# Gate-row loads on ScalarE and GpSimd, sixteen copies on three engines, and a half step more before a visit

## The chip, the cores and the metric

The kernel runs on one core of a Trainium2 chip. The time is device microseconds of one execution; the lower, the better. A profile is one execution taken by the hardware profiler, with a record for each instruction and each DMA packet. In it PE is the tensor engine's matmuls, PEld its weight loads, DVE is VectorE, ACT is ScalarE, POOL is GpSimd, SP is SyncE, and SPq, ACTq and so on are the engines' sequencers (for a DMA: the issue).

## The reference

An attention block without softmax, and on its output a mixture of four experts. All is float32.

```python
def phi(x):                                   # (4, 4, 1088, 32) -> 64 features
    a = einsum('rd,bhsd->bhsr', S1, x)        # S1, S2: (8, 32)
    b = einsum('rd,bhsd->bhsr', S2, x)
    return einsum('bhsi,bhsj->bhsij', a, b).reshape(..., 64)
q_p, k_p = phi(q), phi(k)
kv, z = einsum('bhsf,bhsd->bhfd', k_p, v), k_p.sum(axis=2)
attn = einsum('bhsf,bhfd->bhsd', q_p, kv) / (einsum('bhsf,bhf->bhs', q_p, z) + 1e-6)
x = attn.transpose(0, 2, 1, 3).reshape(4352, 128)
p = domain_probs / (domain_probs.sum(-1) + 1e-9)          # (4352, 4)
out = sum(p[:, e:e+1] * (maximum(x @ w1[e], 0) @ w2[e]) for e in range(4))
# w1: (4, 128, 1024), w2: (4, 1024, 128)
```

## The kernel before

**Tokens and chunks.** The 4352 tokens are cut into eleven chunks: 128, 448, 512, seven of 448, and 128 (`CHUNKS`). For each chunk the expert part runs 16 steps (`NQ`): four experts, four steps each, a step being two blocks of 128 hidden columns. So there are 176 steps, of two half steps each. The first and last chunk are done with plain float32 matmuls in halves (`plain`, L245); chunk 1 uses plain float32 for its first expert (L1102); all the others use three float32r products per block (L1115, L1116, L1164), from weights split into parts (`wa`, `wb`, `wd` by `weight_parts`; `vab`, `vb`, `vd` by `second_weight_parts`) and tokens split into `xa`, `xb`, `xd`. ScalarE takes the relu (`hid` at L1093, L1104, L1172, or `ha` at L1167), VectorE makes the low parts `hb` (L1141) and `hd` (L1144). The second matmuls (`o`, L245, L1213, L1232) follow two steps and more behind.

**Order.** The schedule is written by hand: every engine runs its instructions in the order in which the program emits them, and semaphores make it wait for the others. The main loop is over steps. Work of the attention for later tokens stands as small pieces in a list, `plan`, and `work()` takes pieces from it at each half step, as a credit allows. A piece may have a condition `(name, n)`: it isn't taken before n half steps after the piece `name` ran. `until_there` forces pieces when a chunk's tokens are due.

**The start.** `start()` does the keys and values of the first batch and the first 128 queries (`x_first`), on which the first chunk's step 0 waits. Loads are issued by SP in program order: `S2`, keys `kn`, 128 queries, values `vn` (six loads), 448 queries, `w1` of expert 0, then the gate rows `dp` (three loads, L187) and `ends` (two, L192), then the weights of all experts, the last queries, and the second batch's keys and values. `S1` alone is issued by ScalarE. `gate_sums`, on GpSimd, is the first reader of `dp` and `ends`.

**The second unit.** `queries` and `attend` make the 448 tokens of chunk 1 during chunk 0. Their pieces are `first0` to `first17`: VectorE's shuffles and products (`qp`, L582), the visit on PE (`h<-kvx,qp`), the division, the transpose into `y` (L698), and the copies from `y` to the four row groups of `ring` (L710): sixteen copies of 32 rows and 96 or 128 columns, in two rounds `first16` and `first17`, today on ScalarE (odd heads) and GpSimd (even heads):

```python
copy = nc.scalar.copy if h % 2 else nc.gpsimd.tensor_copy
```

**Later units.** Ten units (`later`) make the rest of the tokens. Each goes: turn on VectorE, projection on PE (`h<-qT,sx`), copy `qs` on ScalarE, out to DRAM and back (`qd`), two products on VectorE (L780), and a visit: the next unit's projection, then this unit's `h<-kvx,qp`. The visit's condition is a number of half steps behind the second product.

Of the kernel before, what the change touches and what calls it, by code (L numbers as in the profile page):

```python
# [17 lines left out]
def _ap(t, p0: int, np_: int, off: int, free):  # L18

    p = list(t.ap)[0]  # L20
    return bass.AP(t.tensor, t.offset + p0 * p[0] + off, [[p[0], np_]] + [list(d) for d in free])
# [3 lines left out]
def kernel(  # L25
# [24 lines left out]
    nc = tc.nc  # L50

    P = 128
    HP = 64
    B, H, S, D = q.shape
    E, DM, F = w1.shape
    R = 8
    R2 = 2 * R
    G = S // 32
# [80 lines left out]
    def load_w1(e):  # L139
        w1_of[e] = cpool.tile([P, F], F32, tag=f"w1_{e}", name="w1_sb")  # L140
        for c in (slice(0, F // 2), slice(F // 2, F)) if e == 1 else (slice(0, F),):
            nc.sync.dma_start(w1_of[e][:, c], w1[e, :, c])

    def load_w2(e, k, to=None):
        of = OTHER if k else THREE
        w2_of[e, k] = cpool.tile([P, len(of) * DM], F32, tag=f"w2_{e}{k}", name="w2_sb")[:, :] if to is None else to
        runs = []
        for b in of:
            if runs and b == runs[-1][1]:
                runs[-1][1] += 1  # L150
            else:
                runs.append([b, b + 1])
        for b, z in runs:
            at = split_at(b)
            nc.sync.dma_start(  # L155
                w2_of[e, k][:, DM * at : DM * (at + z - b)].rearrange("p (g d) -> p g d", d=DM),
                w2[e, P * b : P * z].rearrange("(g p) d -> p g d", p=P),
            )
# [21 lines left out]
    dp = cpool.tile([P, G, E], F32, name="dp")  # L180

    ends = cpool.tile([P, 2, E], F32, name="ends")
    e_sum = cpool.tile([P, 2, 3], F32, name="e_sum")
    load_rows(q, 0, "qn", slice(P, P + UNITS[0][1]))
    load_w1(0)
    for p0, n, g0, m, t in ((0, 96, 0, G, 0), (96, 32, 0, G - 4, 3 * S), (96, 32, G - 4, 4, B * S - P)):
        nc.sync.dma_start(  # L187
            _ap(dp, p0, n, g0 * E, [[1, m * E]]),
            bass.AP(domain_probs.tensor, domain_probs.offset + t * E, [[m * E, n], [1, m * E]]),
        )  # L190
    for i, t, g in ((0, 0, G), (1, B * S - P, 4)):
        nc.sync.dma_start(  # L192
            ends[:, i, :], bass.AP(domain_probs.tensor, domain_probs.offset + t * E, [[g * E, 32], [1, 4 * E]])
        )
    load_w2(0, 0)
    load_w2(0, 1)
    for e in range(1, E):
# [89 lines left out]
    def copy_on(scalar):  # L287
        return nc.scalar.copy if scalar else nc.gpsimd.tensor_copy
# [7 lines left out]
        )  # L296
    for h in range(H):
        copy_on(h > 1)(_ap(sr, 32 * h, 32, 32 * h, [[P, 6], [1, 32]]), _ap(sp, 0, 32, 0, [[32, 6], [1, 32]]))
    mask_lo = [R2 + l % R2 for l in range(32)]
    mask_b = [R + l % R for l in range(32)]  # L300
    mask_a = [[4 * x + l // R for l in range(32)] for x in range(2)]
# [69 lines left out]
    def placed(c, n):  # L371

        for a, z, t, off in PLACES:
            lo, hi = max(c, a), min(c + n, z)
            if lo < hi:
                yield t[:, off + lo - a : off + hi - a], lo - c, hi - lo
# [317 lines left out]
    def attend_out(b, c, n, laid, xs):  # L694

        y = apool.tile([P, QW], F32, tag="y", name="y")
        for c0, T, t0 in laid:
            nc.vector.transpose(  # L698
                _ap(y, 0, P, P * t0, [[32, T[0]], [32 * T[0], H], [1, 32]]),
                _ap(xs, 0, P, P * t0, [[P, T[0]], [D, H], [1, D]]),  # L700
            )
            if b == 0 and c == P:
                for x in range(2):
                    yield
                    for a in (x, x + 2):
                        run = 32 * T[a // 2]
                        for h in range(H):
                            copy = nc.scalar.copy if h % 2 else nc.gpsimd.tensor_copy
                            at = PLACES[1][3] + a // 2 * 64 * T[0] + a % 2 * run
                            copy(ring[32 * h : 32 * h + 32, at : at + run], _ap(y, 32 * a, 32, 32 * T[0] * h, [[1, run]]))  # L710
                continue
            m = 64 * sum(T)
            base = xd.offset + P * (S * b + c + c0)
            for a in range(4):
                run = 32 * T[a // 2]
                nc.sync.dma_start(
                    bass.AP(
                        xd.tensor,
                        base + a // 2 * 64 * T[0] + a % 2 * run,
                        [[m, 32], [32 * m, H], [1, run]],  # L720
                    ),
                    _ap(y, 32 * a, 32, P * t0, [[32 * T[0], H], [1, run]]),
                )
            for to, at, w in placed(S * b + c + c0, m):
                nc.sync.dma_start(to, bass.AP(xd.tensor, base + at, [[m, P], [1, w]]))
        have[0] += n
        yield
# [71 lines left out]
    def add(cost, run, name, after=None):  # L799

        plan.append((cost, run, name, after))

    def lay_plan():

        of_first = queries(0, P, UNITS[0][1])
        costs = [0.62] * 9 + [0.05] * 4 + [0.4, 0.55, 0.6, 0.1, 0.1]
        distances = {12: ("first8", 3), 13: ("first12", 1), 16: ("first15", 2), 17: ("first16", 1)}
        for at, cost in enumerate(costs):
            add(cost, lambda: next(of_first, None), f"first{at}", distances.get(at))
        covers.append((len(plan), P + UNITS[0][1]))  # L810
        add(vector_us(later[0][2]), lambda: unit_turn(0), "qturn", ("start", 2 * NQ - 2))
        add(0.1, lambda: unit_project(0), "visit", ("qturn", 6))
        add(0, lambda: None, "wait", ("start", 2 * NQ + 2))
        keys = {}
        for b in range(1, B):
            now_on, plan[:] = list(plan), []
            key_pieces(b)
            keys[b], plan[:] = list(plan), now_on
        for w, (b, c, n, u) in enumerate(later):
            if b == 0:  # L820
                plan.extend(keys[1][:9])
            else:
                at = {(1, 0): (1, 9, 13), (1, 1): (2, 0, 3), (1, 2): (2, 3, 5), (2, 0): (2, 5, 13)}
                at.update({(2, 1): (3, 0, 3), (2, 2): (3, 3, 9), (3, 0): (3, 9, 13)})
                if (b, u) in at:
                    k, z0, z1 = at[b, u]
                    plan.extend(keys[k][z0:z1])
                if u == 0:
                    key_end(b)
            more = w + 1 < len(later)  # L830
            if more:
                add(vector_us(later[w + 1][2]), lambda w=w: unit_turn(w + 1), "qturn")
            for p in range(2):
                add(vector_us(n), lambda w=w, p=p: unit_product(w, p), "product", ("visit", LAND if w else LAND + 1))

            def visit(w=w, more=more):
                if more:
                    unit_project(w + 1)
                unit_visit(w)

            add(0.1, visit, "visit", ("product", 3 if w < 4 else 2))
            add(0.4, lambda w=w: inverse.__setitem__(w, attend_inverse(*products[w])), "inverse", ("visit", 1))
            add(vector_us(n), lambda w=w: over.__setitem__(w, attend_scale(*products[w], inverse.pop(w))), "scale")
            add(vector_us(n), lambda w=w: unit_out(w), "out")
            covers.append((len(plan), S * b + c + n))
# [3 lines left out]
    def queries(b, c, n):  # L849
        qc = early.pop((b, c))  # L850
        qf = apool.tile([P, QW], F32, tag="qf", name="qf")
        nc.vector.stream_shuffle(in_=qc[:, 0:n], out=qf[:, 0:n], mask=mask_lo)
        yield
        nc.vector.tensor_tensor(out=qf[:, 0:n], in0=qc[:, 0:n], in1=qf[:, 0:n], op=ALU.add)
        free()
        yield
        qb = apool.tile([P, QW], F32, tag="qb", name="qb")
        nc.vector.stream_shuffle(in_=qf[:, 0:n], out=qb[:, 0:n], mask=mask_b)
        yield
        qp = query_tiles()  # L860
        for x in range(2):
            qa = apool.tile([P, QW], F32, tag="qa", name="qa")
            nc.vector.stream_shuffle(in_=qf[:, 0:n], out=qa[:, 0:n], mask=mask_a[x])
            yield
            for p in range(2):
                query_product(qp, p, x, n, qa, qb)
                yield
        yield
        yield
        yield  # L870
        yield from attend(b, c, n, qp)
# [460 lines left out]
    for m in range(1, NC - 1):  # L1332
        at, tokens = NQ * m - 4 if m > 1 else NQ + 1, token_parts(m)
# [45 lines left out]
    for i in range(len(steps) + LA):  # L1379
        if i < len(steps):  # L1380
            m, kq = steps[i]
# [84 lines left out]
```

## Time and profile before

| | us |
|---|---|
| median of three runs (453.1 to 453.74) | 453.47 |
| the profiled execution | 454.41 |
| its span, first to last instruction | 452.6 |

| engine | busy us | share | instructions |
|---|---|---|---|
| PE | 445.4 | 98% | 3013 |
| PEld | 367.8 | 81% | 3013 |
| DVE | 357.0 | 79% | 600 |
| ACT | 332.0 | 73% | 703 |
| POOL | 119.2 | 26% | 206 |

The span is cut into 40 slices of 11.3 us, and each digit is a busy share in tenths: PE shows 8 in the first slice, 7 in the last, and 9 in all others. The granted TensorE clock is full in all. The DMA engines moved 38.45 MB, a mean of 85 GB/s, with up to 283 GB/s in the second slice. In the chain of work that ended last, PE holds 90%, ACT, DMA and the SP queue 2% each.

Rows of the timeline read: start, duration, engine, line, operation, output<-input, shape, count, and in brackets the idle time before the first of them with what ended it. Rows of the same kind that follow each other are merged, so the duration is from the first start to the last end.

### The profile page before, as it was taken

How to read it: one execution, taken by the hardware profiler on the slowest of the kernel's cores; microseconds unless marked ns; L12 is line 12 of the kernel's file. 1: busy time of each engine (PE TensorE's matmuls, PEld its weight loads, DVE VectorE, ACT ScalarE, POOL GpSimd, SP SyncE). 2: the span in 40 equal slices, each digit the busy share in tenths (PEclk: the TensorE clock that was granted, in tenths of full speed). 3: DMA queues.
4: the chain of work that ended last, by engine and by line, in shares of the span. 5: the costliest groups of instructions: out<-in, count | busy, mean ns of one | idle time of the engine just before them, and what ended most of it. 6: DMA issues, size and time to landing. Idle time of an engine off the chain costs nothing.

```text
span 452.6 us, 8664 instructions
## 1 busy us (share of the span) xinstructions
PE 445.4 (98%) x3013; PEld 367.8 (81%) x3013; DVE 357.0 (79%) x600; ACT 332.0 (73%) x703; POOL 119.2 (26%) x206
## 2 busy tenths in 40 slices
PE   8899999999999999999999999999999999999997
PEld 5776678777778888788888888888888888888886
DVE  5868679887988788788877998788779787887753
ACT  4276888777867786688687867787778788878841
POOL 6344133310333123212221232124123212321320
PEclk9999999999999999999999999999999999999999
DMA  6964741114313350151243501320321121017401
GB/s 179 283 172 136 181 123 55 36 23 131 98 46 90 80 136 25 32 135 63 73 116 52 141 22 28 102 67 21 84 61 23 38 45 43 20 37 221 149 2 28
DMA packets 54003, 38.45 MB, mean 85 GB/s; under 512 B 27144, under 2 KB 50120, under 8 KB 53960
## 3 DMA queue, kind: packets, MB, share of 16 engines
q1 hardware_dynamic: 53560, 37.85, 30.9%
q8 instruction: 23, 0.38, 0.3%
q14 instruction: 20, 0.16, 0.1%
q0 software_dynamic: 384, 0.06, 0.1%
q10 hardware_dynamic: 16, 0.00, 0.0%
HBM read 32.68 MB, written 5.21 MB: 84 GB/s over the span
## 4 chain that ended last, share of the span: by engine, by line
PE 90%; ACT 2%; DMA 2%; SPq 2%; DVE 1%; issue 1%; DVEq 0%; ACTq 0%
PE o L1232 39%; PE h L1164 13%; PE h L1115 12%; PE h L1116 12%; PE h L245 7%; PE o L245 2%; PE o L1213 2%; PE h L1102 1%; PE h L430 1%; DMA w_sb<-in_moe_w_dram 1%; SPq L155 1%; DMA vn<-in_v_dram 1%; ACT h L1117 1%; ACT vab L887 0%; ACT ring L710 0%
## 5 line engine op out<-in xcount | busy, mean ns | idle before, releaser
L1117 ACT ACTIVATE h<-h 128x448 f32<-128x448 f32 (+1 forms) x280 | 151.4, 541 | 78.2 <-PE h L1116 73.9
L1141 DVE SCALAR_TENSOR_TENSOR hb<-h,ha 128x448 fp32r<-128x448 f32 (+1 forms) x204 | 125.8, 624 | 53.5 <-ACT ha L1167 52.5
L1115 PE MATMUL h<-xa,wa 128*128 128x448 f32 (+1 forms) x280 | 130.4, 466 | 0.0
L1144 DVE SCALAR_TENSOR_TENSOR hd<-ha,hb 128x896 fp32r<-128x896 f32 (+1 forms) x102 | 116.4, 1141 | 8.5 <-PE h L245 0.5
L1167 ACT ACTIVATE ha<-h 128x448 fp32r<-128x448 f32 (+1 forms) x204 | 111.7, 548 | 0.0
L1164 PE MATMUL h<-xd,wd 128*128 128x448 f32 (+1 forms) x280 | 103.7, 370 | 0.6 <-ACT h L1117 0.6
L1116 PE MATMUL h<-xb,wb 128*128 128x448 f32 (+1 forms) x280 | 103.1, 368 | 0.0
L1271 POOL TENSOR_TENSOR ev<-ev,gate 128x256 f32<-128x256 f32 (+1 forms) x54 | 39.3, 727 | 220.2 <-DVE ev L1264 202.0
L1232 PE MATMUL o<-ha,vab 128*128 128x448 f32 (+1 forms) x204 | 76.3, 374 | 0.0
L1115 PEld LDWEIGHTS h<-xa,wa 128*128 128x128 f32 x280 | 52.7, 188 | 18.7 <-issue 14.3
L1116 PEld LDWEIGHTS h<-xb,wb 128*128 128x128 f32 x280 | 52.7, 188 | 18.6 <-issue 14.8
L1232 PE MATMUL o<-hid,w_sb 128*128 128x448 f32 (+1 forms) x136 | 62.9, 544 | 0.0
L1164 PEld LDWEIGHTS h<-xd,wd 128*128 128x128 f32 x280 | 52.5, 187 | 9.2 <-ACT h L1117 2.7
L1232 PE MATMUL o<-hd,vd 128*128 128x448 f32 (+1 forms) x204 | 58.8, 369 | 0.0
L1232 PE MATMUL o<-hb,vb 128*128 128x448 f32 (+1 forms) x136 | 50.0, 369 | 0.0
L1273 POOL TENSOR_TENSOR total<-total,ev 128x256 f32<-128x256 f32 (+1 forms) x54 | 47.3, 876 | 4.2
L1172 ACT ACTIVATE hid<-h 128x448 f32<-128x448 f32 (+1 forms) x76 | 42.2, 555 | 0.1
L1232 PEld LDWEIGHTS o<-ha,vab 128*128 128x128 f32 x204 | 38.3, 188 | 4.1 <-issue 0.2
L1232 PEld LDWEIGHTS o<-hd,vd 128*128 128x128 f32 x204 | 38.0, 188 | 3.5
L1271 POOL TENSOR_TENSOR total<-ev,gate 128x256 f32<-128x256 f32 (+1 forms) x18 | 12.8, 730 | 78.6 <-issue 58.6
L1232 PEld LDWEIGHTS o<-hid,w_sb 128*128 128x128 f32 x136 | 25.6, 188 | 2.2
L1232 PEld LDWEIGHTS o<-hb,vb 128*128 128x128 f32 x136 | 25.5, 188 | 2.2
(140 smaller groups left out, 451.2 us busy)
## 6 DMA issues: line engine op xcount, KB each, us to landing
gate<-gates SPq DMA_DIRECT2D x24, 224.0 KB
kn<-in_k_dram SPq DMA_DIRECT2D x4, 544.0 KB
vn<-in_v_dram SPq DMA_DIRECT2D x16, 128.0 KB
w_last<-in_moe_w_dram SPq DMA_DIRECT2D x4, 512.0 KB
w_sb<-in_moe_w_dram SPq DMA_DIRECT2D x3, 512.0 KB
w_sb<-in_moe_w_dram SPq DMA_DIRECT2D x6, 256.0 KB
qp<-qd SPq DMA_DIRECT2D x6, 224.0 KB
qb<-qd SPq DMA_DIRECT2D x6, 224.0 KB
```

The lines of the kernel that those rows point to most:

```text
L245: nc.tensor.matmul(out(s), weights(s), moving(s), **flags)
L1115: nc.tensor.matmul(g, wa[:, e, w], xa, start=True, stop=False)
L1116: nc.tensor.matmul(g, wb[:, e, w], xb, start=False, stop=True)
L1117: nc.scalar.activation(g, g, ACTF.Copy, scale=1.0 + R12)
L1141: nc.vector.scalar_tensor_tensor(out=hb, in0=g, scalar=0.0, in1=high, op0=ALU.max, op1=ALU.subtract)
L1144: nc.vector.scalar_tensor_tensor(out=d2, in0=a2.bitcast(F32), scalar=R12, in1=b2.bitcast(F32), op0=ALU.mult, op1=ALU.subtract)
L1164: nc.tensor.matmul(g, w, x, start=False, stop=True, skip_group_check=True)
L1167: nc.scalar.activation(ha, g, ACTF.Relu, scale=NEAR)
L1172: nc.scalar.activation(hid[i][j], g, ACTF.Relu)
L1232: nc.tensor.matmul(acc[m, e][o][:, 0:n], w, h, start=first_one, stop=last)
L1271: nc.gpsimd.tensor_tensor(out=to[:, x], in0=ev[:, x], in1=g[:, x], op=ALU.mult)
L1273: nc.gpsimd.tensor_tensor(out=total[m][:, x], in0=total[m][:, x], in1=ev[:, x], op=ALU.add)
```

## The change

Three edits. First, the five loads of gate rows leave SP's queue, where they stood between the first expert's `w1` and `w2`, and are emitted later in the program, after the copies that build `sr`: the three of `dp` on ScalarE, the two of `ends` on GpSimd. Second, the sixteen copies to `ring` are dealt to VectorE (six), GpSimd (six) and ScalarE (four), and the second round waits two half steps after the first instead of one. Third, the visit of a later unit waits three half steps behind its second product for all units; before it was two for the fifth and later ones.

```diff
     load_rows(q, 0, "qn", slice(P, P + UNITS[0][1]))
     load_w1(0)
-    for p0, n, g0, m, t in ((0, 96, 0, G, 0), (96, 32, 0, G - 4, 3 * S), (96, 32, G - 4, 4, B * S - P)):
-        nc.sync.dma_start(
-            _ap(dp, p0, n, g0 * E, [[1, m * E]]),
-            bass.AP(domain_probs.tensor, domain_probs.offset + t * E, [[m * E, n], [1, m * E]]),
-        )
-    for i, t, g in ((0, 0, G), (1, B * S - P, 4)):
-        nc.sync.dma_start(
-            ends[:, i, :], bass.AP(domain_probs.tensor, domain_probs.offset + t * E, [[g * E, 32], [1, 4 * E]])
-        )
     load_w2(0, 0)
...
     for h in range(H):
         copy_on(h > 1)(_ap(sr, 32 * h, 32, 32 * h, [[P, 6], [1, 32]]), _ap(sp, 0, 32, 0, [[32, 6], [1, 32]]))
+    for p0, n, g0, m, t in ((0, 96, 0, G, 0), (96, 32, 0, G - 4, 3 * S), (96, 32, G - 4, 4, B * S - P)):
+        nc.scalar.dma_start(
+            _ap(dp, p0, n, g0 * E, [[1, m * E]]),
+            bass.AP(domain_probs.tensor, domain_probs.offset + t * E, [[m * E, n], [1, m * E]]),
+        )
+    for i, t, g in ((0, 0, G), (1, B * S - P, 4)):
+        nc.gpsimd.dma_start(
+            ends[:, i, :], bass.AP(domain_probs.tensor, domain_probs.offset + t * E, [[g * E, 32], [1, 4 * E]])
+        )
...
-                            copy = nc.scalar.copy if h % 2 else nc.gpsimd.tensor_copy
+                            at = "vgsvgvsg"[a // 2 * H + h]
+                            copy = {"v": nc.vector.tensor_copy, "g": nc.gpsimd.tensor_copy, "s": nc.scalar.copy}[at]
...
-        distances = {12: ("first8", 3), 13: ("first12", 1), 16: ("first15", 2), 17: ("first16", 1)}
+        distances = {12: ("first8", 3), 13: ("first12", 1), 16: ("first15", 2), 17: ("first16", 2)}
...
-            add(0.1, visit, "visit", ("product", 3 if w < 4 else 2))
+            add(0.1, visit, "visit", ("product", 3))
```

## The prediction

> **What bounds the kernel now.** I read the summary of busy time first (PE 445.4 of 452.6 us, granted clock 1.000 throughout), so only a stretch in which PE stands still can be won. The next view is who PE waited for. Its three lines that this change can reach:
>
> ```profile
> PE h L245 <- DMA w_sb<-in_moe_w_dram: 0.9, 1, 0.9
> PE o L245 <- ACT hid L1093: 0.7, 1, 0.7
> PE h L245 <- DVE qp L780: 0.3, 1, 0.3
> ```
>
> Columns: total us, times, longest. A PE row ends later than the next could start (a 128-column row shows 0.27 us, yet back to back they start 0.04 to 0.07 apart), so I price each stall from start to start. The timeline, first around 20 us:
>
> ```profile
> 19.71 0.62 DVE L582 TENSOR_TENSOR qp<-qa,qb 64x448 f32<-64x448 f32 x1
> 20.36 0.35 DVE L1196 TENSOR_SCALAR end<-o,ends 128x128 f32<-128x128 f32 x1
> 20.73 0.62 DVE L582 TENSOR_TENSOR qp<-qa,qb 64x448 f32<-64x448 f32 x1
> 21.22 0.66 PE L245 MATMUL h<-x_first,w_sb 128*64 128x128 f32 x8 [0.94 <-DMA w_sb<-in_moe_w_dram]
> 21.68 1.13 PE L245 MATMUL h<-kvx,qp 128*64 128x66 f32 x32
> 22.61 0.64 PE L245 MATMUL o<-w_sb,hid 128*64 128x128 f32 x8
> ```
>
> The row before 21.22 starts at 20.01; the next was due at 20.07. PE lost 1.15 us waiting for the third expert's first weights (step 8). Then ScalarE's copies:
>
> ```profile
> 25.07 2.35 ACT L710 COPY ring<-y 32x128 f32<-32x128 f32 x8
> 27.44 0.66 ACT L1093 ACTIVATE hid<-h 128x256 f32<-128x256 f32 x2
> 27.88 0.66 PE L245 MATMUL o<-w_sb,hid 128*64 128x128 f32 x8 [0.70 <-ACT hid L1093]
> ```
>
> Eight copies in a row hold back a `hid` that PE wants at 26.95: 0.93 us. Third, the visit of the fifth unit:
>
> ```profile
> 189.36 0.42 DVE L780 TENSOR_TENSOR qp<-qp,qb 128x256 f32<-128x256 f32 x1
> 189.83 0.45 PE L245 MATMUL h<-kvx,qp 128*64 128x66 f32 x8 [0.26 <-DVE qp L780]
> ```
>
> The row before starts at 189.34, so 0.49 less the usual 0.03: 0.46 us. From 300 us on PE repeats one expert of a 448-column chunk every 10.02 us, and visits add only their own work; nothing later takes back time won earlier, as due times count half steps and move with PE. The most to be had is 1.15 + 0.93 + 0.46 = 2.54 us.
>
> **Part 1, the gate loads leave SP.** The issue queue shows what stood ahead of those weights:
>
> ```profile
> 5.58 0.35 SPq L109 DMA_DIRECT2D qn<-in_q_dram  x1
> 5.98 0.43 SPq L142 DMA_DIRECT2D w_sb<-in_moe_w_dram  x1
> 6.47 1.34 SPq L187 DMA_DIRECT2D dp<-in_moe_domain_probs_dram  x3
> 7.86 1.31 SPq L192 DMA_DIRECT2D ends<-in_moe_domain_probs_dram  x2
> 9.21 3.06 SPq L155 DMA_DIRECT2D w_sb<-in_moe_w_dram  x4
> 15.28 0.43 SPq L142 DMA_DIRECT2D w_sb<-in_moe_w_dram  x1
> ```
>
> Removed: 1.34 + 1.31 us and gaps, 9.21 - 6.47 = 2.74 us of SP. That would put the issue at 15.28 (landing 21.09) at 12.54. But it does not come whole. The built program's waits show that the issues of SP and ScalarE share eight semaphores in rotation, each waiting for the transfer eight places before. With `dp` on ScalarE three things shift. The fourth `vn` load, once free at 3.52, waits for `kn`, whose landing released the 5.58 issue; so SP issues that `vn` at 5.58, two more to about 6.95, then `qn` to 7.4. The first weights wait for the first `dp` load, the next two for the other two. ScalarE comes to them at 5.76, after its `sr` copies; `s_raw`, its only load so far, was issued at 0.74 and used at 2.39, 1.65 us later, and on engines as busy as here (share 0.9 to 1.1 from 5 to 9 us) I add 0.5: the first lands at 7.9. So the first weights go out at 7.9 instead of 5.98 (PE needs them at 13.80; to the last packet they took 3.4 us), the next at 8.4 and 8.9 instead of 9.21 and 10.79. At 9.2 comes a stretch that stays: the 9.21 issue took 1.53 us instead of 0.45, as did those at 16.23 and 23.88 (1.25, 1.17), each beside a 16 KB instruction fetch of 1.0 to 1.15 us, and these follow PE's progress. After it SP is one to two issues ahead, 0.5 to 1.0 us, and I take 0.75: issue at 14.5, landing at 20.35. Bounds: the DMA engines are idle from 9.4 to 11.4 and near 0.95 busy from 12 to 20, so not more than 1.9 us earlier; and with `dp` landing at 9.3 instead of 7.9, as late behind a queue as `vn` (issued 3.52, landed 7.82), 0.6 later than now.
>
> The page "DMA: Bandwidth & Descriptors" of the Trainium skill, section "Issuing engines are not separate DMA queues", says that loads from any engine end on the same 16 DMA engines, and another issuer saves only issue time. The share of 0.97 from 15 to 20 us agrees for that stretch; the hole at 10 us is issue time, and by the rule it alone can be won.
>
> What is late next: the visit's products. VectorE works without a pause to 21.35 (rows above), whatever PE does. PE needs `qp0` for the first 16 rows of `h<-kvx,qp` and `qp1` for the other 16, which began at 22.16. They can begin at 21.40 at the earliest. So of 1.15 us only 22.16 - 21.40 = 0.76 is there, in full if the weights land by 20.35. I take 0.70 (0 to 0.76, and to -0.6 if the landing slips).
>
> The loads' new places: ScalarE stood idle from 5.76 to 7.37; three issues at 0.42 (SP's) to 0.58 (its own, `s_raw`) end at 7.1 to 7.65. A `fs` copy 0.28 late is caught by VectorE's 0.18 wait before its third product and by PE's own queue: 0 to 0.1. POOL stood idle from 5.80 to 7.89; its twelve gate stores:
>
> ```profile
> 31.82 7.13 POOL L341 DMA_DIRECT2D gates<-pt  x12 [1.06 <-DVE end L1200]
> ```
>
> are 0.58 each, first one 0.77, so the two end at 7.2. If POOL's products start by 8.9 PE loses nothing: key sums run 0.128 us a block from 9.61, the fifth block wants POOL's first two products (1.21 us) at 10.12. The rows here have 128 pieces and not 40, so up to 1.85 each if that scales: start at 9.5, loss 0.6. SP's own rows (0.65 against 0.72 for the 40-piece stores) don't scale, so I take 0. `ends` land by about 11, when POOL wants them (11.68).
>
> **Part 2, sixteen copies dealt.** Per round VectorE 3, POOL 3, ScalarE 2; the instruction order shows ScalarE: two copies, `hid`, two copies, `hid`. A copy is 0.29, a `hid` 0.39: in the old frame 25.07 to 25.65, `hid` to 26.05 (wanted 26.95), copies and `hid` to 27.04 (wanted 27.87). The whole 0.93 goes. VectorE's six copies come in its 3.71 us of idle before 28.79 at 0.2 to 0.25 each (a 32x64 transpose took 0.23): 1.5 us, then the weights' splits earlier than now. POOL: six of 0.31 instead of eight. The ring is whole near 27, before, and PE reads it at 30.21, then 28.6. If VectorE's copies also held POOL's for their 1.5 us it would still be in time. Nothing is taken off: 0.93 (0.7 to 0.93).
>
> **Part 3, one half step more.** It binds for the last six of the ten units. A half step is 10.02/8 = 1.25 us; the product that ended at 189.78 then beats PE's row at about 190.6. The order moves four visits by a half step, three later and one (320 columns) earlier; only the fifth unit's stalled, so 0.46 is the gain, and 0 to 0.5 the cost of VectorE's changed order around `hb` and `hd` elsewhere. I take 0.46.
>
> **Sum.** 0.70 + 0.93 + 0.46 = 2.09 us off the profiled run: 454.41 to 452.3 (span 450.5). That run lies 0.94 above the median of the runs; the same off 453.47 gives 451.4.
>
> **Rivals.**
> - The rotation eats part 1: the weights land no earlier than 21.09. For: the new waits on `dp`. Against: the hole at 10 us. 453.47 - 0.93 - 0.46 = 452.1; with the slip of 0.6, 452.7. Chance 0.2.
> - The half step moves the stall (VectorE's backlog at 184 to 190 us stays, `hd` waits next): part 3 gives nothing, 451.9, or costs 0.5, 452.4. Chance 0.13.
> - Slower: POOL's products start late. Its two loads stand ahead of the set-up of its product code, which today hides in 5.80 to 7.89; later than 8.9 each us goes onto PE's path to 13.80, and past 11.0 the gain of 2.09 is gone. From the row, set-up is at most 2.1: 7.2 + 2.1 = 9.3, a loss of 0.4. But where the loads are 1.85 each and the set-up whole 2.1, it starts at 11.6: loss 2.7, 454.1. If they only wait out VectorE's transposes (to 7.27), 10.5: loss 1.6, 453.0. Against: the twelve stores kept 0.58 while VectorE was busy 4.96 of 5 us. Chance 0.07, of it 0.02 for a time inside 0.2%. The page "GPSIMD Engine Reference", section "Instruction dispatch", puts a first call of fresh code at about 6 us; the first product here starts 2.1 us after POOL's last copy, so the trace disagrees. By that figure alone the estimate would be a start at 7.2 + 6 = 13.2, a loss of 4.3 and 455.7; I leave it 0.02 of the 0.07.
>
> **Numbers.** Forecast 0.60. Range 450.8 (all 2.54 and a little) to 453.0 (first two rivals whole). 0.2% is 0.9 us, about what a measurement tells here: faster means below 452.56. Faster: the forecast, most of the second rival and two thirds of the first, less some mixing of the small losses: 0.81. Same: the rest of those and part of the third, 0.14. Slower: 0.05 of the third.
>
> **What would show it.** Right: PE's wait for `w_sb` gone or under 0.4, with a wait of some 0.3 for `qp` in its place; the first weights issued near 7.9; no wait for `hid` near 27; PE at its first `ring` row near 28.6; no PE wait for a 128x256 product; `x_first` still met at 13.80. Wrong: PE's first expert row later than 13.9, the third expert's weights landing after 21, or a new VectorE wait after 180 us.

## The result, and the profile after

The changed kernel takes 452.39 us in the median of 13 runs (452.23 to 452.77), the kernel before 453.62 us (13 runs, 453.1 to 454.14). The ratio is 0.9974, with a 95% interval of 0.9965 to 0.9983. So the kernel is 1.2 us faster (0.8 to 1.6). The forecast was 451.4, the range 450.8 to 453.0.

The two profiled executions say more than that: 452.55 us with a span of 450.6 after, against 454.41 and 452.6 before. That is 2.0 us of span, close to the forecast's 2.09. Why the runs show only 1.2 is what most of the experiments ask.

Who PE waited for in the changed kernel (total us, times, longest; L245 of before is L236 here, L387 and L582 are the same, and lines from L710 on are one higher):

```profile
PE h L1165 <- ACT h L1118: 0.6, 2, 0.3
PE h L236 <- DVE kT L387: 0.5, 1, 0.5
PE h L236 <- DVE qp L582: 0.2, 1, 0.2
```

The three waits that the change could reach, for `w_sb`, for `hid` at 27 us and for the product at 189 us, are gone. A new one of 0.2 for `qp` of L582 stands in the place of the first. The timeline shows it:

```profile
20.02 0.61 PE L236 MATMUL h<-x_first,w_sb 128*64 128x128 f32 x8
20.26 0.35 DVE L1197 TENSOR_SCALAR end<-o,ends 128x128 f32<-128x128 f32 x1
...
20.62 0.62 DVE L582 TENSOR_TENSOR qp<-qa,qb 64x448 f32<-64x448 f32 x1
...
21.30 0.69 PE L236 MATMUL h<-kvx,qp 128*64 128x66 f32 x16 [0.21 <-DVE qp L582]
```

PE meets the third expert's weights without a pause (20.02 instead of 21.22), and then stands before the second half of the visit until VectorE's last product ends at 21.24. The copies, next:

```profile
24.08 1.82 POOL L711 COPY ring<-y 32x128 f32<-32x128 f32 x6 [8.53 <-DVE y L698]
24.18 1.80 DVE L711 COPY ring<-y 32x128 f32<-32x128 f32 x6
24.25 0.58 ACT L711 COPY ring<-y 32x128 f32<-32x128 f32 x2
...
24.85 0.38 ACT L1094 ACTIVATE hid<-h 128x256 f32<-128x256 f32 x1
...
26.19 0.61 PE L236 MATMUL o<-w_sb,hid 128*64 128x128 f32 x8
```

ScalarE makes two copies, then a `hid`; PE's row that was held to 27.88 starts at 26.19. And the queue that issues the loads:

```profile
7.29 0.44 SPq L142 DMA_DIRECT2D w_sb<-in_moe_w_dram  x1
8.01 1.92 SPq L155 DMA_DIRECT2D w_sb<-in_moe_w_dram  x4
9.98 0.90 SPq L142 DMA_DIRECT2D w_sb<-in_moe_w_dram  x2
10.93 3.19 SPq L155 DMA_DIRECT2D w_sb<-in_moe_w_dram  x4
14.15 0.43 SPq L142 DMA_DIRECT2D w_sb<-in_moe_w_dram  x1
```

The third expert's weights are issued at 14.15 instead of 15.28. The hole in the DMA engines' work at 10 us is closed. A row of the table by stretch, first of before, then of after (start:end, length, busy us and counts of the engines, clock, DMA share, GB/s):

```profile
10.00:12.00 2.00, 2.00 (x70) 1.89 (x65) 1.90 (x8) 0.19 (x2) 1.50 (x9) 1.00 0.21 59
```

```profile
10.00:12.00 2.00, 2.00 (x67) 1.80 (x62) 1.90 (x7) 0.10 (x1) 1.71 (x10) 1.00 1.07 333
```

A share of 0.21 became 1.07. The visit that the third part moves now has its sixteen rows in one piece, where before had eight, a wait and eight:

```profile
188.82 0.64 PE L236 MATMUL h<-kvx,qp 128*64 128x66 f32 x16
```

In PE's rows, after minus before, the difference is -0.09 us at 18 us, ahead of the three waits, -0.84 at the second half of the visit at 21 us, -1.69 after the copies, and -2.1 at the end: all three parts did what they were meant to do in this pair of profiles.

### The profile page after: what moved, and what is told of

Read it like the earlier page. It is cut to its first block, busy times and chain, and to the rows that moved or that the text cites. A ratio compares the mean times of both kernels' runs of the same rounds, so it can differ in the third digit from the quotient of the medians.

```text
span 450.6 us, 8662 instructions
## 1 busy us (share of the span) xinstructions
PE 445.1 (99%) x3013; PEld 367.7 (82%) x3013; DVE 359.4 (80%) x606; ACT 330.7 (73%) x699; POOL 120.3 (27%) x206
## 4 chain that ended last, share of the span: by engine, by line
PE 93%; DVE 3%; ACT 2%; DMA 1%; issue 1%; SPq 0%; ACTq 0%; DVEq 0%
PE o L1233 40%; PE h L1165 13%; PE h L1116 13%; PE h L1117 13%; PE h L236 7%; PE o L236 3%; PE o L1214 2%; PE h L1103 1%; DMA vn<-in_v_dram 1%; PE h L430 1%; DVE qp L582 1%; ACT h L1118 1%; ACT vab L888 0%; DVE qa L864 0%; ACT hid L1173 0%
```

## The experiments

Every kernel is timed against the kernel before on the same chip.

**The kernel before again, and each part alone.** The first is the file of before; the next three apply one of the diff's three edits each.

> The kernel before, unchanged. The profiles of the two kernels differ by 2.0 us of span (452.6 to 450.6), the medians of the runs by only 1.2 (453.62 to 452.39). Theory A (a late draw): the profiled execution of before was a slow one, since its 454.41 lies above all 13 other runs of it (453.1 to 454.14); then the spans here lie around 451.8, median 453.6, and the stalls that the prediction priced from that one profile are smaller in the usual execution, most likely the DMA one (PE waiting for w_sb, 0.9 there), because it hangs on when a transfer lands. Theory B (the profile is typical, something outside the span differs): the spans here are 452.5 to 452.7 again and the part of the time that lies around the span is about 1.0 us instead of 1.81. Ratio to before 1.000 in both.

> Part 1 alone: the five loads of gate rows on ScalarE and GpSimd, the copies and the visits as before. The prediction priced it at 0.70 us (0.84 was seen between the two profiles): 453.62 - 0.70 = 452.9. Theory A (the DMA stall is smaller in the usual execution of before): 0 to 0.3 us gained, 453.3 to 453.6. Theory B: 0.70 to 0.84, 452.8 to 452.9. In both the profile shows no wait for w_sb near 20 us, a wait of about 0.2 for the product of L582, the first weights issued near 7.3, and the third expert's near 14.2; the wait for hid of 0.7 near 26 us and that for the product of L780 near 189 stay.

> Part 2 alone: the sixteen copies to ring dealt to three engines and the second round two half steps behind the first; loads and visits as before. The prediction priced it at 0.93 us: 453.62 - 0.93 = 452.7, and both theories leave that term alone, since engine work and not a transfer sets it. If copies and DMA stall depend on each other (a later PE start makes the copies' hold shorter), less: 0.5, 453.1. The profile should show no wait for hid near 27 us, the wait for w_sb near 20 us unchanged (0.9 in the one profile so far).

> Part 3 alone: the visits of the fifth and later units three half steps behind their second product; loads and copies as before. The prediction priced it at 0.46 us: 453.62 - 0.46 = 453.2. Rival: the half step moves the stall or VectorE's changed order costs elsewhere, 0 gained or 0.5 lost, 453.6 to 454.1. The profile should show no wait for the product of L780 near 189 us and PE 0.4 to 0.5 us ahead of before from there to the end. If the sum of the three parts alone is near 1.2 us, the whole has lost nothing; if it is near 2.1, the parts hinder each other in the usual execution.

Measured against 453.81 us:

| | median us | ratio (95%) | median span |
|---|---|---|---|
| e1_before_again | 453.87 | 0.9997 (0.9988 to 1.0006) | 452.1 |
| e2_loads_only | 453.70 | 0.9998 (0.9989 to 1.0007) | 451.9 |
| e3_copies_only | 453.23 | 0.9985 (0.9976 to 0.9994) | 451.4 |
| e4_visit_only | 453.47 | 0.9994 (0.9986 to 1.0003) | 451.7 |

Theory A holds. Over 85 runs of before in these experiments the median span is 451.9 (451.4 to 452.9), and only two have 452.6 or more, the span of the profile that the prediction read. The time around the span stays near 1.8 us in both kernels, so theory B falls. A part of the draw can be seen in PE's row for the third expert, in the profiles of e1_before_again, then of e4_visit_only, whose loads are those of before:

```profile
20.69 0.66 PE L245 MATMUL h<-x_first,w_sb 128*64 128x128 f32 x8 [0.75 <-DMA w_sb<-in_moe_w_dram]
```

```profile
21.24 0.66 PE L245 MATMUL h<-x_first,w_sb 128*64 128x128 f32 x8 [1.14 <-DMA w_sb<-in_moe_w_dram]
```

Seven profiles have the gate loads on SP: before and six experiments. I took single rows from them: the time from the last `h<-x_first` row ahead of the wait to the seventeenth `h<-kvx,qp` row. With the gate loads moved it is 1.82 or 1.83 in all five profiles in which `end` stands where it was. What lies above 1.82 is what part 1 can take:

| profile | weights issued | PE's row starts | stretch | above 1.82 |
|---|---|---|---|---|
| before | 15.28 | 21.22 | 2.58 | 0.76 |
| e1_before_again | 15.15 | 20.69 | 2.38 | 0.56 |
| e3_copies_only | 14.80 | 20.70 | 2.11 | 0.29 |
| e4_visit_only | 15.37 | 21.24 | 2.77 | 0.95 |
| e6_distance_only | 14.86 | 20.22 | 1.94 | 0.12 |
| e7_deal_only | 14.80 | 20.25 | 1.84 | 0.02 |
| e10_no_part1 | 15.08 | 21.09 | 2.39 | 0.57 |

The mean is 0.47 us, and before's profile is the second highest.

The start is a draw too. Before's profile differs from that of e1_before_again, the same kernel, by 0.50 us of span. Of this 0.34 is there already in PE's first row of step 0 (13.80 against 13.46), and 0.19 comes with the wait for `w_sb`. The 0.34 begins at VectorE's first `kT<-kn` row, which waits for the keys' transfer: it starts at 5.59 and 5.26 in these two, and between 5.12 and 5.59 in all fourteen profiles.

In e2_loads_only the wait is gone as expected, with this in its place:

```profile
21.43 0.69 PE L236 MATMUL h<-kvx,qp 128*64 128x66 f32 x16 [0.21 <-DVE qp L582]
```

The three gains alone, 0.11, 0.58 and 0.34 us, add to 1.03, within the interval of the whole (0.8 to 1.6): no loss between the parts shows, though each of the three is known only to about 0.4 us.

Of part 2, e3_copies_only's profile has the term almost whole at first. Against e1_before_again, which met the weights at the same time, PE is 0.90 us ahead at 27 us. At 171 us it gives 0.2 back. PE's weight load waits for VectorE's `ev`, and the `hd` ahead of that had started late (both rows from that profile, of two engines):

```profile
168.43 1.09 DVE L1145 SCALAR_TENSOR_TENSOR hd<-ha,hb 128x896 fp32r<-128x896 f32 x1 [0.46 <-PE h L1117]
```

```profile
170.10 0.30 PEld L1233 LDWEIGHTS o<-hid,w_sb 128*128 128x128 f32 x2 [0.33 <-DVE ev L1265]
```

All nine profiles with copies on VectorE have this idle time of 0.46 before `hd`, and the five without such copies (before, e1, e2, e4 and e6) have none. The bracket names the PE row whose semaphore came last, here `h<-xb,wb`, which ended at 168.32; in the five others `hd` starts before that row has ended. That PE row need not be the cause: it ends 0.10 to 0.13 us ahead of `hd`, while the time since VectorE's own `hb` (done at 167.97) is 0.46 in all nine to within 0.002. Why `hd` starts only at 168.43 stays open.

Of part 3, e4_visit_only's PE is 0.54 us behind e1_before_again at first (0.16 from the start, 0.38 from the weights' draw), 0.07 behind from 192 us on, and 0.17 behind at the end: 0.47 won at the visit, 0.10 given back between 214 and 325 us, 0.37 left. The 0.10 can't be put down to the changed order: between the profiles of after and e9_after_again, the same kernel, a lead of 0.24 at 22 us shrinks to 0.02 by the end, most of it between 80 and 280 us.

**The two halves of part 2, on the kernel before.** e6 changes only the distance, e7 only the engines.

```diff
-        distances = {12: ("first8", 3), 13: ("first12", 1), 16: ("first15", 2), 17: ("first16", 1)}
+        distances = {12: ("first8", 3), 13: ("first12", 1), 16: ("first15", 2), 17: ("first16", 2)}
```

> Half of part 2 on the kernel before: the second round of copies two half steps behind the first, all copies on ScalarE and GpSimd as before (four of 0.29 in a row on ScalarE, twice). Theory D (the distance alone is enough: a hid of ScalarE comes between the two rounds): four copies from 25.07 end at 26.24, the hid is done by 26.65, ahead of PE's 26.95; no wait for hid, and the same gain as all of part 2, 0.58 us, 453.2. Theory E (dealing is needed): four copies in a row still hold one hid back by 0.2 to 0.5, gain 0.3 or less, 453.5.

> The other half of part 2 on the kernel before: the copies dealt to three engines, the second round one half step behind the first as before. If ScalarE's two copies of each round run with no hid between them, four of 0.29 hold it 1.17 us instead of 2.35, from 25.07 to 26.24, and hid follows by 26.65, ahead of PE: no wait and the whole 0.58 us, 453.2. If the dealing and the distance are both needed, a wait for hid of 0.2 to 0.4 stays near 27 us, 453.5.

Against 453.57 us: e6_distance_only 453.50 (0.9997, 0.9989 to 1.0006), e7_deal_only 452.96 (0.9986, 0.9977 to 0.9995). Theory E is the nearer one on the distance: in the times it alone brings nothing that can be measured (-0.3 to 0.5 us). The rows of ScalarE and PE in e6's profile say why it is not enough:

```profile
25.70 1.16 ACT L710 COPY ring<-y 32x128 f32<-32x128 f32 x4
26.88 0.38 ACT L1093 ACTIVATE hid<-h 128x256 f32<-128x256 f32 x1
```

```profile
27.32 0.66 PE L245 MATMUL o<-w_sb,hid 128*64 128x128 f32 x8 [0.24 <-ACT hid L1093]
```

The first four copies let a `hid` pass, but the second four, at 1.16 us, hold the next one. In that profile the distance still wins 0.43 us (PE against before's is 0.95 ahead at 24 us, 1.38 at 30), about half of the 0.90 of all of part 2; the interval of the times holds both 0 and 0.43. Dealing alone is worth 0.61 us: ScalarE's four copies run in a row from 24.13 to 25.29 there, and the `hid` rows behind them are still in time.

**VectorE's cap, and the waits that remain.** e5 moves the first `end` (VectorE) of the changed kernel behind the last product, by holding it until the next call of `behind`. e8 starts two weight splits earlier.

```diff
-    for e, at, then in zip((1, 2, 3, 0), (12, 13, 16, 19), (32, 17, 20, 23)):
+    for e, at, then in zip((1, 2, 3, 0), (12, 13, 16, 17), (32, 17, 20, 22)):
```

> The changed kernel with one VectorE instruction moved: the first expert's scaling by the gate row (`end`, 0.35 us at 20.26 in the profile of after) is emitted behind the last product of L582 instead of ahead of it. Theory C (VectorE caps part 1): in the changed kernel the weights have landed and PE waits for that product alone, at 21.30; with the product 0.36 earlier the second half of h<-kvx,qp starts at 20.93 to 20.95, PE is 0.3 to 0.37 ahead of the changed kernel from there on, span 450.2 to 450.3. Rival (the weights or the next reader cap it as well): the start stays at 21.1 or later, or PE gives the time back before 30 us, span 450.6. In the times 0.35 us is 0.08%, less than they can tell alone: 452.0 to 452.4 beside before at 453.7.

> The changed kernel with the two waits that stay in its profile attacked: PE waits for ScalarE at 50.27 and at 61.62 (start to start 0.47 and 0.45 us lost), each time behind a weight split of ScalarE (wa at 49.12 behind vab at 48.39; vab at 58.98). The splits of expert 0's first weights begin two steps earlier (17 instead of 19) and those of its second weights one step earlier (22 instead of 23). If ScalarE has room there (idle 0.75 us before 37.28, 1.06 before 42.01), both waits go: 0.9 us, span 449.7, 451.5. If the earlier splits hold back another relu, or VectorE, full from 28 to 34 us, holds the new order, less: 0 to 0.4 us, 452.0 to 452.4; worse than 452.4 only if a plain step of the first expert is stalled.

In e5_end_late the cap is gone: the 32 rows of `h<-kvx,qp` run from 20.53 without a break, and the stretch of the table falls from 1.82 to 1.46 us, 0.36 as expected. The time is 452.19 (0.9969, 0.9958 to 0.9981), not to be told from the changed kernel's. In the profile the 0.36 us does not last: 0.28 goes between 68 and 70 us, where ScalarE's `xa` (68.79) waits 0.16 for the transfer `ring<-xd`, the same place as in e8's rows below, and some 0.24 more in small steps up to 322 us, as much as the two profiles of the changed kernel (after and e9) drift against each other there.

In e8_splits_earlier (451.92; 0.9965, 0.9953 to 0.9977) both waits go, and PE is 0.72 us ahead of the changed kernel's profile at 61.6, 0.12 of it from the start. Then 0.35 comes back as a new wait. ScalarE's split of the next chunk's tokens stands in its queue for a transfer, and PE waits for the relu behind it:

```profile
68.52 0.63 ACT L888 ACTIVATE xa<-ring 128x512 fp32r<-128x512 f32 x1 [0.31 <-DMA ring<-xd]
...
69.64 0.47 PE L1165 MATMUL h<-xd,wd 128*128 128x448 f32 x1 [0.20 <-ACT h L1118]
```

**Part 1 undone, and a better kernel.** e9 is the changed kernel again, e10 has parts 2 and 3 only. e11 is e8 with the split of chunk 2's tokens a step later; e12 is e11 with e5's edit.

```diff
-        at, tokens = NQ * m - 4 if m > 1 else NQ + 1, token_parts(m)
+        at, tokens = (NQ + 1, NQ * m - 3, NQ * m - 4)[min(m, 3) - 1], token_parts(m)
```

> The changed kernel, unchanged, beside the three others of this call on the same chip. Its spans of 13 runs were 450.3 to 451.0; expected 450.6, ratio to before 0.997 (1.2 us). If its profile again meets no wait for w_sb and starts the second half of h<-kvx,qp at 21.3, the landing of the weights no longer decides.

> The changed kernel with part 1 undone: the five loads of gate rows on SP again, copies and visits as changed. Theory A (the weights land in draws about 0.5 us apart, at PE starts of 20.2, 20.7 or 21.2, and part 1 takes only what lies behind VectorE's cap of 21.4 for the second half of h<-kvx,qp): 0.1 to 0.3 us slower than the changed kernel in the median, 452.5 to 452.7 where that has 452.4, and a wider spread of spans, about 1 us against 0.7. Theory of the prediction (part 1 worth 0.70): 453.1.

> The kernel with the splits earlier, and the split of chunk 2's tokens one step later (29 instead of 28). In the profile of e8_splits_earlier PE came 0.72 us ahead at 61.6 and gave 0.35 back at 69.64, where ScalarE had stood behind its split xa of the tokens, which waited for their transfer (ring<-xd) to 68.5. Theory F (that transfer is what took it back): with the split a step later PE keeps 0.7 or more, span 449.8 or less, 0.3 us below e8. Rival (the relu behind the split is late in the next step as well, or VectorE, full there, is late with xb): no difference from e8, 451.9.

> All of it: the changed kernel, the first expert's scaling behind the products (e5), the splits earlier (e8) and the tokens' split a step later (e11). If the three gains add: 0.28 + 0.7 us off the changed kernel, 451.3 to 451.5, ratio to before 0.995. If the early 0.28 us is taken back in the middle as in e5's profile, 451.7.

| | median us (runs) | ratio to before, 453.75 us (95%) | median span |
|---|---|---|---|
| e9_after_again | 452.36 (452.31 to 452.99) | 0.9972 (0.9962 to 0.9982) | 450.6 |
| e10_no_part1 | 452.74 (452.37 to 453.16) | 0.9981 (0.9972 to 0.9990) | 451.0 |
| e11_splits_tokens | 451.84 (451.59 to 451.94) | 0.9958 (0.9945 to 0.9970) | 450.1 |
| e12_all | 451.65 (451.49 to 452.15) | 0.9956 (0.9944 to 0.9969) | 449.7 |

Part 1 is worth 452.74 - 452.36 = 0.38 us beside the other two. That lies between theory A's 0.3 and the prediction's 0.70, nearer to A, and agrees with the mean of 0.47 from the table. It is not sharp: the runs of the two overlap, and their intervals against before do too. In e9's profile PE again met the weights without a wait and began the second half of `h<-kvx,qp` at 21.06. The spread did not widen as A expected (spans 450.6 to 451.3 in e10, 450.3 to 451.2 in e9). In e11_splits_tokens no wait for a relu is left in PE's list, as theory F says; but the time differs from e8's, taken on another chip, by less than the intervals, so what the step alone brings to the time is not measured. In the profiles PE wins 0.47 us on e8's between 69.6 and 70 us. e12_all beats both kernels: its runs lie wholly below those of the changed kernel on the same chip, by 0.7 us in the median. Its waits:

```profile
PE h L236 <- DVE kT L387: 1.1, 1, 1.1
PE h L224 <- PEq L1460: 0.8, 1, 0.8
PE h L236 <- DVE kvz L475: 0.2, 1, 0.2
```

Nothing behind the start is left.

## Why the prediction was right, and where its sum was off

**The direction and the mechanisms** were right. All three waits went; the 0.3 us wait for `qp` came as 0.2; `x_first` was met at 13.71 (13.80 before); the first `ring` row started at 28.47 (28.6 foreseen).

**The step that was mis-sized is the base of the sum.** The prediction took its stalls from one execution and took them off the median of the runs, though it had noted that this execution lay 0.94 us above that median. A part of the 0.94 was the stall it was pricing, 0.76 there against 0.47 in the mean; another was the late start of that execution (0.34 against e1's profile), which no part could win. For part 1 the term of 0.70 was right for that profile (0.76 by the table, 0.84 in the pair of profiles, 0.09 of it from the start), but the seven profiles spread from 0.02 to 0.95 with a mean of 0.47, and the runs show 0.11 (e2, alone) and 0.38 (e9 against e10). Sum of the terms as the runs had them: 0.38 for part 1 and 453.75 - 452.74 = 1.01 for parts 2 and 3 together, 1.39 in all, against 2.09. A smaller slip: a block's first row follows 0.10 behind the row before it where nothing waits (19.92 and 20.02 in the profile of after), not 0.04 to 0.07, so the first two stalls were 1.11 and 0.89, not 1.15 and 0.93.

**Part 1's working.** The weights were issued at 14.15 (14.5 foreseen). The first ones went out at 7.29, not 7.9, because ScalarE's issue of `dp` began at 5.05 and not behind its copies at 5.76. So the rotation held the first weights back by 1.31 us, but the third expert's went out 1.13 earlier than before, and the first rival did not come. The cap by VectorE's product was right: 21.30 against 21.40, and e5 shows that moving the product lifts it. The page "DMA: Bandwidth & Descriptors" of the Trainium skill, section "Issuing engines are not separate DMA queues", would have another issuer save issue time alone; the trace agrees, since the share of 0.21 at 10 us became 1.07 while from 14 us on it was near 1 in both kernels.

**Part 2's term** of 0.93 was 0.90 at 27 us in the profile and 0.58 to 0.61 in the runs. The claim that nothing later takes back time won earlier failed here: 0.2 us went at 171 us. VectorE's copies took 0.30 each (1.80 for six), not 0.20 to 0.25; the ring was whole in time all the same.

**Part 3's term** of 0.46 was 0.47 at the visit, 0.37 at the end of the profile and 0.34 in the runs, though that last interval holds zero (-0.1 to 0.6). The cost of 0 to 0.5 for VectorE's changed order, which the forecast set to nothing, is at most the 0.10 given back behind the visit in that profile, and that is within the drift between two executions of one kernel.

**The slower rival**, POOL's set-up behind its two loads, did not come. Those loads ended at 7.04 and the first product began at 7.80, 0.09 earlier than before, held by ScalarE's `fs`:

```profile
5.74 1.30 POOL L296 DMA_DIRECT2D ends<-in_moe_domain_probs_dram  x2
7.80 1.20 POOL L452 TENSOR_TENSOR kp<-fs 128x256 f32<-128x256 f32 x2 [0.76 <-ACT fs L419]
```

The page "GPSIMD Engine Reference", section "Instruction dispatch", of the Trainium skill names about 6 us for the first call of freshly loaded code; here there are at most 0.76 us between the loads and the product, so the trace shows no such time. Whether the product's code counts as fresh there, no run shows.

## What to carry to other kernels

A stall that a transfer ends is a draw: read it in several executions, or look at where the profiled one lies among the runs, before its length goes into a sum; what lies above the median there may be the very stall, or another transfer at the start that the change does not touch. A wait can only be won down to the next releaser, so name that one and its time. On an engine that takes its instructions in order, fewer instructions in a row ahead of an urgent one can matter more than where the next batch of them is put.

## What was not expected of the hardware

- ScalarE issued DMAs beside its own copies: the `dp` issues ran from 5.05 to 6.32, while copies filled 5.04 to 5.75.
- The same transfer, issued between 14.80 and 15.37, let PE start 5.36 to 6.01 us later in seven profiles, and the starts lie near 20.2, 20.7 and 21.1 to 21.2. What makes these steps was not found.
- VectorE's `hd` near 168 us starts after 0.46 us of idle in each of the nine profiles with VectorE copies, 140 us behind the last of them, and in none of the five without. The cause was not found.
